# A decay attention and two MLPs on one core: buffers, loads and copies of the attention stage rearranged

## The chip, the cores and the metric

One Trainium2 chip, one of its cores. The metric is the device time of one execution in microseconds, the median of several runs; lower is better. TensorE (PE) multiplies, VectorE (DVE), ScalarE (ACT) and GpSimd (POOL) do the element work, SyncE (SP) issues most transfers. Each engine runs its own instructions in order and waits on semaphores for the others.

## What is computed

Twelve chunks of 64 positions go through a linear attention with decay, for 2 batches and 8 heads; its output is the input of two MLPs of 2048 hidden units. All in float32.

```python
for b in range(nb):                                  # 12 chunks of 64 positions
    intra = (einsum('bhic,bhjc->bhij', qb, kb) * Dmask) @ vb
    inter = einsum('bhid,bhde->bhie', qb * lam_pow, kv_state)
    out[:, :, chunk] = intra + inter
    kv_state = lam_block * kv_state + einsum('bhsd,bhse->bhde', kb * rev_pow, vb)
x = out as (1536 tokens, 512)
h = x @ w_in;  x = (h * clip(h + 3, 0, 6) / 6) @ w_out       # first MLP
h = x @ w_in2; out = maximum(0.01 * h, h) @ w_out2           # second MLP
```

## The kernel before

**Layout.** The two batches lie on the two halves of the partitions: `own[b]` are the 64 partitions of batch b, `other[b]` the rest (lines 155 and 156). The hidden states lie in three groups of 512 tokens, `t` = 0, 1, 2; four chunks of both batches make a group (`SPT` = 4).

**The order.** Nothing is issued as it is written. Each step is added to a list with `add(engine and modelled us, function, due, after, takes, frees)` (line 52). `Order.issue` (line 59) then plays a model of the engines: a step may start when its `after` steps are done in the model, the buffers that it takes are free and its engine is idle; among those that may start, the earliest due goes first, dues being carried back along `after`. The instructions are written in that order, and on the chip each engine keeps it, whatever it waits for. SP's transfers are one such engine ("dma"), so a load that waits for a buffer holds up all loads behind it.

**The attention, chunk by chunk** (lines 242 to 362). `load_qk` brings queries, keys and keys by position, three transfers of 128 partitions, into one of `NQ` = 4 places in the tile `sums`. `load_v` brings the values of two chunks into a tile `vs` (3 buffers) of 128 partitions, two chunks, two slots; both transfers write slot 0 on all 128 partitions. `part_v` then copies the half of batch 1 from slot 0 to slot 1, ScalarE for chunks 0 to 2, VectorE for the others, and `state_copy` puts the running state on the partitions left over, so that one matmul takes values and state at once. `queries` copies queries to PSUM beside the scores (two copies), `scores` is 32 small matmuls, `mask` multiplies by the decay on VectorE, `k_decay` scales keys on GpSimd, `state` and `attn_out` are 32 small matmuls each, and `att_x` splits the output in PSUM into a high part (a cast on ScalarE) and a low part (a difference on VectorE), because the later products take each operand as high and low. A place for queries is free again when scores, query copies and scaled keys of its chunk are done; a value tile when the outputs and states of both of its chunks are done.

**After the attention.** The weights come as raw 64-bit words (`load_w`, 3 buffers) and are turned into high and low parts by ScalarE and VectorE (`low_bits` to `w_low`). The first blocks of the first MLP are done tile by tile. From the third block on, groups 0 and 1 are multiplied by a scheme with seven products instead of eight, which needs differences of the inputs, T1 to T4. `sums_1` (line 877) makes them: `x_whole` (line 620) adds high and low parts back to the whole, four times on VectorE, `x_diff` subtracts, and `x_split` splits again. They lie in a tile of the pool `s`, which opens when the attention's pools close (`open_late`, line 584); the products' sums of weights use the same pool.

Of the kernel before, what the change touches and what calls it, by code (L numbers as in the profile page):

```python
# [40 lines left out]
NQ = 4  # L41
# [75 lines left out]
def decay_attention_two_mlps(ctx: ExitStack, tc: tile.TileContext, qkk, vv, lam, w1, w2, out):  # L117
# [3 lines left out]
    sizes = {"raw": 3, "cv": 3, "cl": 2, "w0": 4, "w1": 5, "st": 2, "G": 3, "u": 3, "h": 2, "a": 2, "r": 3, "vs": 3}  # L121
    late = {"s": 2, "Gx": 3, "ux": 3}
# [125 lines left out]
    def load_v(c):  # L248

        def fn(_):  # L250
            vp = new("vs", [P, 2, 2, H, D], F32)
            VS[c], VS[c + 1] = vp[:, 0], vp[:, 1]
            for i in range(2):
                nc.sync.dma_start(out=vp[:, i, 0], in_=vv[c + i])
            if c == 0:
                nc.gpsimd.memset(vp[other[1], 0, 1], 0.0)
        return fn

    def part_v(c):

        def fn(e):
            (nc.scalar.copy if e == "act" else nc.vector.tensor_copy)(out=VS[c][own[1], 1], in_=VS[c][own[1], 0])  # L262
            if c == 0:
                nc.gpsimd.memset(VS[0][other[0], 0], 0.0)
        return fn
# [62 lines left out]
    x_ready = {}  # L328
    ld = {}
    for c in range(NSC):  # L330
# [3 lines left out]
        ld["v", c] = add(("act", 0.6) if c < 3 else ("dve", 0.5), part_v(c), d - 1.0, after=[ld["vp", c]])  # L334
    st, copies, masks, dense_ops, att_ops = {}, {-1: []}, [], [op_warm], []
    for c in range(NSC):
# [11 lines left out]
        if not last:  # L348
            st[c] = add(pe, state(c), d + 1.3, after=ks + [ld["v", c]] + copies[c - 1] + ([op_rows[c % 2]] if c else []),
                        takes=["a"])  # L350
            copies[c] = [add(("act", 0.58), state_copy(c, b), after=[st[c], ld["v", c + 1]]) for b in range(2)]
            add(("none", 0.0), nothing, after=copies[c], frees=["a"])
        o = add(pe, attn_out(c), d + 2.6, after=[m, ld["v", c]] + copies[c - 1], takes=["h"])
# [5 lines left out]
        x_ready[c] = add(("dve", 0.69), att_x(c, True), d + 5.0, after=[hi], frees=["h"])  # L359
# [86 lines left out]
    composed, low, s_at = {}, {}, {}  # L446
    for l in range(2):
        for f in range(NF):
            for j in range(2):
                h = (l, f, j)  # L450
                held = paired(l, f) and j == 0
                ld_w = add(("dma", 1.45), load_w(h), takes=["raw"])
# [7 lines left out]
            if paired(l, f) and f % 2:  # L460
# [3 lines left out]
                hi = s_at[l, p] = add(("act", 1.05), s_high(l, p), after=[i], takes=["s"])  # L464
# [115 lines left out]
    XT, CS, SPARE = {}, {}, {}  # L580
# [23 lines left out]
    def spare(k, n):  # L604
        i = {"B11": 0, "T1": 0, "B12": 1, "T3": 1, "B22": 2, "T2": 2, "B21": 3, "T4": 3}[n]
        return SPARE[k, 0][:, i] if k else SPARE[k, i // 2][:, i % 2]
# [4 lines left out]
    def x_split(k, n, lo, src):  # L611
# [6 lines left out]
        return fn  # L618

    def x_whole(k, n):  # L620
        def fn(_):
            if n == "B11" or n == "B22" and not k:
                SPARE[k, int(n == "B22")] = pool["s"].tile([P, 2 << k, 2, TT >> k], F32, tag="s", name=f"x_spare{k}")
            x = [part([x[i].bitcast(F32) for x in X], k, n) for i in range(2)]
            nc.vector.tensor_tensor(out=spare(k, n), in0=x[0], in1=x[1], op=ALU.add)
# [249 lines left out]
    last_whole = {}  # L875

    def sums_1(k):
        u, ts = ("dve", 0.61 * (2 - k)), (2, 2) if k else PAIR
        for n, t in (("B11", 0), ("B21", 0), ("B22", 1)):
            x_op[0, k, n] = x_of(ts[t])  # L880
        w = {}
        for n, t in (("B11", 0), ("B12", 1), ("B22", 1), ("B21", 0)):
            w[n] = last_whole[0] = add(u, x_whole(k, n), after=[op_late, last_whole.get(0), *x_of(ts[t])],
                                       takes=["s"] * (n == "B11" or n == "B22" and not k))
        t1 = add(u, x_diff(k, "T1", "B12", "B11", spare), after=[w["B11"], w["B12"]])
        t3 = add(u, x_diff(k, "T3", "B22", "B12", spare), after=[t1, w["B22"]])
# [128 lines left out]
```

## Time and profile before

| | |
|---|---|
| median of 3 runs | 565.16 us (564.86 to 566.2) |
| the profiled execution | 564.53 us |
| its span, first to last instruction | 562.4 us |
| TensorE busy | 548.1 us, 97% |
| VectorE busy | 415.8 us, 74% |
| ScalarE busy | 356.7 us, 63% |
| transfers | 61.66 MB, mean 110 GB/s |
| granted TensorE clock | 0.999 of full speed |

The span is what the trace shows; some 2 us of the execution lie around it. A busy share is a mean over stages with different limits, so the views by stage are read beside it. A timeline row in brackets tells how long the engine sat idle before the instruction and what ended that; "issue" there, and in the chain, is time in which the engine waited for nothing that the profile shows. The DMA share is the mean busy share of the 16 transfer engines; packets that overlap can put it above 1.

### The profile page before, as it was taken

The numbers are of one execution on the slowest core, as the hardware profiler recorded it, in microseconds if no ns is written. First come the engines' busy times: TensorE is split into PE (matmuls) and PEld (weight loads), VectorE is DVE, ScalarE is ACT, GpSimd is POOL, SyncE is SP. The second block draws the span as 40 slices with busy tenths as digits, with TensorE's granted clock in tenths as the row PEclk, the third lists the DMA queues.
The fourth block names the chain that finished last, engine by engine and source line by source line (L and its number), as shares of the span: only waits on it lengthen the run. The fifth ranks groups of instructions, "written<-read, shape, count | busy, mean of one in ns | idle before, by whom it ended". The sixth has DMA issues, their size and how long they took to land.

```text
span 562.4 us, 9066 instructions
## 1 busy us (share of the span) xinstructions
PE 548.1 (97%) x3504; PEld 457.6 (81%) x3504; DVE 415.8 (74%) x693; ACT 356.7 (63%) x625; POOL 68.2 (12%) x78
## 2 busy tenths in 40 slices
PE   8889999999999999999999999999999999999996
PEld 5778888888888888888888888888888888888885
DVE  7868999989888985787689897686368943782332
ACT  5688885658656845578675886686268825683111
POOL 6561001101011101101000000000110110110000
PEclk9999999999999999999999999999999999999999
DMA  8992334247066434534200402141443622512332
GB/s 310 350 334 100 113 112 94 41 133 201 9 160 153 129 81 107 131 113 93 76 1 1 161 27 85 66 150 38 94 87 119 168 59 45 128 46 43 75 76 75
DMA packets 25436, 61.66 MB, mean 110 GB/s; under 512 B 2994, under 2 KB 2994, under 8 KB 25394
## 3 DMA queue, kind: packets, MB, share of 16 engines
q1 hardware_dynamic: 18592, 48.77, 26.2%
q0 software_dynamic: 6480, 11.80, 12.4%
q8 instruction: 27, 0.44, 0.3%
q10 hardware_dynamic: 322, 0.52, 0.3%
q14 instruction: 15, 0.12, 0.1%
HBM read 46.14 MB, written 3.15 MB: 88 GB/s over the span
## 4 chain that ended last, share of the span: by engine, by line
PE 95%; DMA 2%; issue 1%; DVE 1%; SPq 0%; DVEq 0%
PE acc L552 46%; PE h L639 20%; PE a L639 11%; PE h L482 6%; PE a L482 6%; PE h L315 2%; PE a L303 2%; PE pair L278 2%; DMA vs<-vv 2%; PE a L552 1%; DVE sums L565 0%; SPq L245 0%; DVE r L294 0%; DVE vs L262 0%; DVE a L671 0%
## 5 line engine op out<-in xcount | busy, mean ns | idle before, releaser
L525 POOL DMA_DIRECT2D sums<-st x45 | 39.4, 908 | 423.7 <-ACT st L563 408.4
L552 PE MATMUL acc<-Gh,wh 128*128 128x512 f32 x136 | 53.0, 390 | 0.0
L552 PE MATMUL acc<-Gl,wh 128*128 128x512 f32 x136 | 52.9, 389 | 0.0
L552 PE MATMUL acc<-Gh,wl 128*128 128x512 f32 x136 | 52.9, 389 | 0.0
L552 PE MATMUL acc<-wl,Gh 128*128 128x512 f32 x128 | 50.0, 391 | 0.0
L552 PE MATMUL acc<-wh,Gh 128*128 128x512 f32 x128 | 50.0, 391 | 0.0
L552 PE MATMUL acc<-wh,Gl 128*128 128x512 f32 x128 | 49.8, 389 | 0.0
L387 ACT ACTIVATE c<-raw 128x512 uint32<-128x512 uint32 x64 | 42.8, 670 | 6.4 <-DVE t L410 4.6
L410 DVE CUSTOM_DVE_ANT_0 t<-t,c 128x1024 uint16<-128x1024 uint16 x64 | 45.0, 704 | 2.2
L408 DVE SCALAR_TENSOR_TENSOR t<-raw,t 128x512 uint32<-128x512 uint32 x64 | 44.1, 689 | 1.1
L420 DVE TENSOR_TENSOR wl<-t,wh 128x512 fp32r<-128x512 f32 (+1 forms) x64 | 41.4, 652 | 2.2 <-ACT wh L416 2.0
L391 ACT ACTIVATE t<-raw 128x512 f32<-128x512 f32 x64 | 42.8, 669 | 0.0
L511 DVE TENSOR_TENSOR Gl<-u,Gh 128x512 fp32r<-128x512 f32 x32 | 22.1, 689 | 25.7 <-ACT Gh L689 25.5
L416 ACT CAST wh<-t 128x512 fp32r<-128x512 f32 (+1 forms) x64 | 37.7, 594 | 3.6 <-DVE t L410 2.8
L563 ACT COPY st<-acc 128x512 f32<-128x512 f32 x43 | 25.2, 588 | 22.9 <-PE acc L552 16.3
L639 PE MATMUL h<-xh,s 128*128 128x512 f32 x112 | 38.4, 389 | 0.0
L397 DVE TENSOR_SCALAR t<-t 128x512 f32<-128x512 f32 x64 | 27.0, 421 | 14.6 <-ACT t L391 14.6
L695 ACT ACTIVATE u<-a 128x512 f32<-128x512 f32 x24 | 14.3, 597 | 30.9 <-PE a L639 30.9
L565 DVE TENSOR_TENSOR sums<-acc,sums 128x512 f32<-128x512 f32 x27 | 18.5, 690 | 20.3 <-PE acc L552 20.2
L508 DVE SCALAR_TENSOR_TENSOR Gl<-u,Gh 128x512 fp32r<-128x512 f32 x36 | 24.6, 686 | 8.7 <-ACT Gh L501 8.6
L552 PEld LDWEIGHTS acc<-Gh,wh 128*128 128x128 f32 x136 | 25.5, 188 | 5.4
L552 PEld LDWEIGHTS acc<-Gh,wl 128*128 128x128 f32 x136 | 25.5, 188 | 5.4
(181 smaller groups left out, 1482.2 us busy)
## 6 DMA issues: line engine op xcount, KB each, us to landing
raw<-w SPq DMA_DIRECT2D x58, 512.0 KB, 3.3
sums<-st POOLq DMA_DIRECT2D x45, 256.0 KB, 3.9
sums<-qkk SPq DMA_DIRECT2D x36, 256.0 KB, 5.5
vs<-vv SPq DMA_DIRECT2D x12, 256.0 KB, 5.0
raw<-w SPq DMA_DIRECT2D x12, 256.0 KB, 3.7
out<-sums SPq DMA_DIRECT2D x20, 128.0 KB, 2.4
out<-sums ACTq DMA_DIRECT2D x4, 128.0 KB, 3.2
lam_sb<-lam ACTq DMA_DIRECT2D x1, 0.0 KB
```

What stands on the lines that cost most here:

```text
L387: nc.scalar.activation(out=CV[h][1], in_=RAW[h][:, :, 0], func=AF.Copy, scale=2.0 ** -29)
L391: return lambda _: nc.scalar.activation(out=CV[h][0].bitcast(F32), in_=RAW[h][:, :, 1].bitcast(F32), func=AF.Abs)
L397: nc.vector.tensor_scalar(out=t.bitcast(F32), in0=t.bitcast(F32), scalar1=MAG_MIN, scalar2=MAG_MAX, op0=ALU.max, op1=ALU.min)
L408: nc.vector.scalar_tensor_tensor(out=t, in0=RAW[h][:, :, 1], scalar=0xC0000000, in1=t, op0=ALU.bitwise_and, op1=ALU.bitwise_or)
L410: nc.vector.tensor_tensor(out=t, in0=t, in1=c, op=ALU.add)
L416: nc.scalar.copy(out=W[h][0][:, cols(*h)], in_=CV[h][0].bitcast(F32)[:, cols(*h)])
L420: return lambda e: eng[e].tensor_tensor(out=W[h][1][:, cols(*h)], in0=CV[h][0].bitcast(F32)[:, cols(*h)], in1=W[h][0].bitcast(F32)[:, cols ...
L482: nc.tensor.matmul(ps, a[:, ws], x[:, k, :], start=(n == 0), stop=(n == 3 * KC - 1))
L525: return lambda _: nc.gpsimd.dma_start(out=SUM[t][:, e, :], in_=STAGE[t, e], accum_op=ALU.add)
L552: nc.tensor.matmul(ACC[e], a, x, start=(first and n == 0 and not seeded(s, e)), stop=(last and n == 2), skip_group_check=seeded(s, e))
L563: nc.scalar.copy(out=STAGE[t, e], in_=ps)
L639: nc.tensor.matmul(ps, ws[a][:, c * P:(c + 1) * P], xs[b][:, c], start=(first and n == 0), stop=(n == 5), skip_group_check=True)
```

## The change

- `NQ` goes from 4 to 3, the value tiles `vs` from 3 to 2.
- The pool `s` opens at the start instead of after the attention.
- `load_v` writes the half of batch b of both chunks straight into slot b: two transfers of 64 partitions by two chunks, instead of two of 128 partitions. `part_v` goes; what waited for it waits for the load.
- `att_spare` is new: for the chunks of groups 0 and 1 ScalarE copies the attention output in PSUM a second time, whole, into a tile of `s`. The PSUM buffer is free when low part and whole copy are done. `x_whole` goes, and `sums_1` starts from these copies.
- Loads of raw weights are bound behind loads of queries: the first behind chunk 8, the second behind chunk 10, all others behind chunk 11.

The core of the diff:

```diff
@@ -38,7 +38,7 @@
 N_DENSE = {("s", 0): 5, ("t", 0): 2, ("o", 0): 2}
-NQ = 4
+NQ = 3
 
@@ -118,8 +118,8 @@
 
-    sizes = {"raw": 3, "cv": 3, "cl": 2, "w0": 4, "w1": 5, "st": 2, "G": 3, "u": 3, "h": 2, "a": 2, "r": 3, "vs": 3}
-    late = {"s": 2, "Gx": 3, "ux": 3}
+    sizes = {"raw": 3, "cv": 3, "cl": 2, "w0": 4, "w1": 5, "st": 2, "s": 2, "G": 3, "u": 3, "h": 2, "a": 2, "r": 3, "vs": 2}
+    late = {"Gx": 3, "ux": 3}
     const = ctx.enter_context(tc.tile_pool(name="const", bufs=1))
@@ -250,18 +250,10 @@
             VS[c], VS[c + 1] = vp[:, 0], vp[:, 1]
-            for i in range(2):
-                nc.sync.dma_start(out=vp[:, i, 0], in_=vv[c + i])
-            if c == 0:
-                nc.gpsimd.memset(vp[other[1], 0, 1], 0.0)
-        return fn
-
-    def part_v(c):
-
-        def fn(e):
-            (nc.scalar.copy if e == "act" else nc.vector.tensor_copy)(out=VS[c][own[1], 1], in_=VS[c][own[1], 0])
-            if c == 0:
-                nc.gpsimd.memset(VS[0][other[0], 0], 0.0)
+            for b in range(2):
+                nc.sync.dma_start(out=vp[own[b], :, b], in_=vv[c:c + 2, own[b]].rearrange("c p h d -> p c h d"))
+                if c == 0:
+                    nc.gpsimd.memset(vp[other[b], 0, b], 0.0)
         return fn
@@ -325,13 +317,23 @@
 
-    x_ready = {}
+    SPARE = {}
+
+    def att_spare(c):
+        def fn(_):
+            j, i = divmod(c, SPT)
+            if not i:
+                SPARE[j] = pool["s"].tile([P, 2, 2, TT], F32, tag="s", name="x_spare")
+            x = SPARE[j].rearrange("p j k (c b i) -> p (j k) c b i", c=SPT, b=2)[:, :, i]
+            nc.scalar.copy(out=x, in_=PA["o", c])
+        return fn
+
+    x_ready, spared = {}, {}
     ld = {}
...
         ld["vp", c] = ld["vp", c - 1] if c % 2 else add(("dma", 1.4), load_v(c), d if c else 0.0, after=[ld["qk", c]], takes=["vs"])
-        ld["v", c] = add(("act", 0.6) if c < 3 else ("dve", 0.5), part_v(c), d - 1.0, after=[ld["vp", c]])
     st, copies, masks, dense_ops, att_ops = {}, {-1: []}, [], [op_warm], []
@@ -346,17 +348,20 @@
         if not last:
-            st[c] = add(pe, state(c), d + 1.3, after=ks + [ld["v", c]] + copies[c - 1] + ([op_rows[c % 2]] if c else []),
+            st[c] = add(pe, state(c), d + 1.3, after=ks + [ld["vp", c]] + copies[c - 1] + ([op_rows[c % 2]] if c else []),
                         takes=["a"])
-            copies[c] = [add(("act", 0.58), state_copy(c, b), after=[st[c], ld["v", c + 1]]) for b in range(2)]
+            copies[c] = [add(("act", 0.58), state_copy(c, b), after=[st[c], ld["vp", c + 1]]) for b in range(2)]
             add(("none", 0.0), nothing, after=copies[c], frees=["a"])
-        o = add(pe, attn_out(c), d + 2.6, after=[m, ld["v", c]] + copies[c - 1], takes=["h"])
+        o = add(pe, attn_out(c), d + 2.6, after=[m, ld["vp", c]] + copies[c - 1], takes=["h"])
         add(("none", 0.0), nothing, after=[o, st.get(c)], frees=["vs"] * (c % 2) + ["r"])
...
         hi = add(("act", 0.58), att_x(c, False), d + 4.0, after=[o])
-        x_ready[c] = add(("dve", 0.69), att_x(c, True), d + 5.0, after=[hi], frees=["h"])
+        x_ready[c] = add(("dve", 0.69), att_x(c, True), d + 5.0, after=[hi])
+        if c < 2 * SPT:
+            spared[c] = add(("act", 0.58), att_spare(c), d + 5.0, after=[hi], takes=["s"] * (not c % SPT))
+        add(("none", 0.0), nothing, after=[x_ready[c], spared.get(c)], frees=["h"])
         att_ops += [x_ready[c], m, o, *ks, *copies.get(c, []), *([st[c]] if c in st else [])]
@@ -443,13 +448,14 @@
 
-    composed, low, s_at = {}, {}, {}
+    AFTER_QK = {(0, 0, 0): NSC - 4, (0, 0, 1): NSC - 2}
+    composed, low = {}, {}
     for l in range(2):
...
                 held = paired(l, f) and j == 0
-                ld_w = add(("dma", 1.45), load_w(h), takes=["raw"])
+                ld_w = add(("dma", 1.45), load_w(h), after=[ld["qk", AFTER_QK.get(h, NSC - 1)]], takes=["raw"])
                 a = add(("act", 0.67), low_bits(h), after=[ld_w], takes=["cv", "cl"])
@@ -461,7 +467,7 @@
                     i = add(("dve", 0.43), w_sum(l, p, n), after=[composed[l, f - 1, 0], composed[l, f, 0], i])
-                hi = s_at[l, p] = add(("act", 1.05), s_high(l, p), after=[i], takes=["s"])
+                hi = add(("act", 1.05), s_high(l, p), after=[i], takes=["s"])
                 s_ready[l, p] = add(("dve", 1.22), s_low(l, p), after=[hi], frees=["raw"])
@@ -577,7 +583,7 @@
 
-    XT, CS, SPARE = {}, {}, {}
+    XT, CS = {}, {}
     A_B = (("A11", "B11"), ("S1", "T1"), ("S2", "T2"), ("A12", "B21"), ("S3", "T3"), ("S4", "B22"), ("A22", "T4"))
@@ -602,8 +608,8 @@
     def spare(k, n):
-        i = {"B11": 0, "T1": 0, "B12": 1, "T3": 1, "B22": 2, "T2": 2, "B21": 3, "T4": 3}[n]
-        return SPARE[k, 0][:, i] if k else SPARE[k, i // 2][:, i % 2]
+        i = {"B11": 0, "T1": 0, "B21": 1, "T4": 1, "B12": 2, "T3": 2, "B22": 3, "T2": 3}[n]
+        return SPARE[i // 2][:, i % 2]
 
@@ -615,14 +621,6 @@
                 nc.scalar.copy(out=xh, in_=src(k, n))
-        return fn
-
-    def x_whole(k, n):
-        def fn(_):
-            if n == "B11" or n == "B22" and not k:
-                SPARE[k, int(n == "B22")] = pool["s"].tile([P, 2 << k, 2, TT >> k], F32, tag="s", name=f"x_spare{k}")
-            x = [part([x[i].bitcast(F32) for x in X], k, n) for i in range(2)]
-            nc.vector.tensor_tensor(out=spare(k, n), in0=x[0], in1=x[1], op=ALU.add)
         return fn
@@ -872,24 +870,18 @@
 
-    last_whole = {}
-
-    def sums_1(k):
-        u, ts = ("dve", 0.61 * (2 - k)), (2, 2) if k else PAIR
+    def sums_1():
+        u = ("dve", 1.22)
         for n, t in (("B11", 0), ("B21", 0), ("B22", 1)):
-            x_op[0, k, n] = x_of(ts[t])
-        w = {}
-        for n, t in (("B11", 0), ("B12", 1), ("B22", 1), ("B21", 0)):
-            w[n] = last_whole[0] = add(u, x_whole(k, n), after=[op_late, last_whole.get(0), *x_of(ts[t])],
-                                       takes=["s"] * (n == "B11" or n == "B22" and not k))
-        t1 = add(u, x_diff(k, "T1", "B12", "B11", spare), after=[w["B11"], w["B12"]])
-        t3 = add(u, x_diff(k, "T3", "B22", "B12", spare), after=[t1, w["B22"]])
-        t2 = add(u, x_diff(k, "T2", "B22", "T1", spare), after=[t3])
-        t4 = add(u, x_diff(k, "T4", "B21", "T2", spare), after=[t2, w["B21"]])
-        for n, after in (("T1", [t2]), ("T2", [t4]), ("T4", [t4]), ("T3", [t3, last1[0, ts[1]]])):
-            splits(0, k, n, after, spare)
-        done = [x_op[0, k, n][0] for n in ("T1", "T3", "T2", "T4")]
-        for d in (done,) if k else (done[:2], done[2:]):
+            x_op[0, 0, n] = x_of(PAIR[t])
+        t1 = add(u, x_diff(0, "T1", "B12", "B11", spare), after=list(spared.values()))
+        t3 = add(u, x_diff(0, "T3", "B22", "B12", spare), after=[t1])
+        t2 = add(u, x_diff(0, "T2", "B22", "T1", spare), after=[t3])
+        t4 = add(u, x_diff(0, "T4", "B21", "T2", spare), after=[t2])
+        for n, after in (("T1", [t2]), ("T2", [t4]), ("T4", [t4]), ("T3", [t3, last1[0, PAIR[1]]])):
+            splits(0, 0, n, [op_late, *after], spare)
+        done = [x_op[0, 0, n][0] for n in ("T1", "T4", "T3", "T2")]
+        for d in (done[:2], done[2:]):
             add(("none", 0.0), nothing, after=d, frees=["s"])
@@ -964,8 +956,7 @@
 
-    sums_1(0)
-    od.ops[s_at[0, starts[0][SINGLE] // 2]][3].append(last_whole[0])
+    sums_1()
     for b in range(SINGLE, len(BLOCKS[0])):
```

## Rows read from the trace of the kernel before

**Rows 1.** Busy time by stage: stretch, length, each engine, clock, DMA share, GB/s.
```profile
0.00:50.00 50.00, 42.07 (x989) 34.70 (x990) 40.35 (x55) 34.94 (x61) 28.86 (x33) 1.00 0.84 297
50.00:400.00 350.00, 350.00 (x1720) 291.07 (x1719) 289.35 (x489) 243.72 (x421) 25.35 (x29) 1.00 0.34 95
```

**Rows 2.** Chain of waits, 0 to 62 us: start, length in us, what.
```profile
15.69 0.88 issue
...
18.62 1.08 PE a L303 x32
...
20.89 1.66 issue
...
31.18 1.22 issue
...
41.30 0.96 issue
...
42.59 1.08 PE a L303 x32
...
46.59 0.97 issue
...
48.01 2.98 PE h L482 x12
```

**Rows 3.** Timeline of TensorE, one block: start, us, what, idle time before it.
```profile
36.92 0.33 PE L315 MATMUL h<-r,vs 128*64 128x64 f32 x2 [0.28 <-issue]
37.18 1.15 PE L278 MATMUL pair<-sums 64*64 64x64 f32 x32
38.26 1.15 PE L303 MATMUL a<-vs,kd 128*64 128x64 f32 x32
39.24 1.10 PE L315 MATMUL h<-r,vs 128*64 128x64 f32 x32
40.27 1.02 PE L278 MATMUL pair<-sums 64*64 64x64 f32 x27
```

**Rows 4.** The page: busy time, a transfer queue, one line of the DMA issues.
```profile
PE 548.1 (97%) x3504; PEld 457.6 (81%) x3504; DVE 415.8 (74%) x693; ACT 356.7 (63%) x625; POOL 68.2 (12%) x78
...
q8 instruction: 27, 0.44, 0.3%
...
vs<-vv SPq DMA_DIRECT2D x12, 256.0 KB, 5.0
```

**Rows 5.** Busy time by stage again: first loads, stores on one queue, on two.
```profile
2.00:24.00 22.00, 18.59 (x385) 13.64 (x385) 18.10 (x26) 13.71 (x24) 14.04 (x13) 1.00 1.03 371
544.10:545.90 1.80, 1.80 (x12) 1.38 (x11) 0.38 (x1) 0.00 (x0) 0.00 (x0) 1.00 0.95 205
557.80:558.30 0.50, 0.00 (x0) 0.00 (x0) 0.18 (x1) 0.00 (x0) 0.00 (x0) 1.00 1.04 389
```

**Rows 6.** Timeline of SP's transfer queue: start, us to issue, what, how many.
```profile
33.64 0.80 SPq L254 DMA_DIRECT2D vs<-vv  x2
34.48 2.01 SPq L380 DMA_DIRECT2D raw<-w  x2
```

**Rows 7.** Timeline of ScalarE, one chunk in the attention.
```profile
28.12 1.19 ACT L308 COPY vs<-a 64x512 f32<-64x512 f32 x2 [0.48 <-PE a L303]
29.21 0.58 ACT L325 CAST xh<-h 128x512 fp32r<-128x512 f32 x1
29.82 1.20 ACT L286 COPY pair<-sums 64x512 f32<-64x512 f32 x2
```

**Rows 8.** Lines 262 and 625 (ns min/median/max), and a timeline row of TensorE.
```profile
L262 DVE COPY vs<-vs x9: 419/425/1281, 12.7 to 45.6; 64x512 f32<-64x512 f32 x9
L262 ACT COPY vs<-vs x3: 614/616/616, 6.2 to 12.5; 64x512 f32<-64x512 f32 x3
...
L625 DVE TENSOR_TENSOR x_spare<-xh,xl x4: 1217/1220/1220, 63.3 to 97.4; 128x1024 f32<-128x1024 f32 x4
...
9.98 1.15 PE L303 MATMUL a<-vs,kd 64*64 64x64 f32 x32 [0.74 <-POOL kd L268]
```


## What the change is expected to do

> **What bounds the kernel now.** I read the table by stage first. From 50 to 400 us TensorE is busy in all 350.00 of 350.00 us, in 0 to 50 us only 42.07 of 50 [rows 1]. What the change does to VectorE, ScalarE and the loads can therefore move the end only through the first 50 us, where 7.9 us lie open. Everything after is a fixed train of matmuls, which starts earlier or later.
>
> Next I read the chain of waits of that stretch. It shows where the open time lies: the chain runs over TensorE alone, and the holes are called "issue", 0.88, 1.66, 1.22, 0.96 and 0.97 us [rows 2], with one of 0.28 more [rows 3], together 5.97 us. No semaphore explains them, and they fall inside groups of 32 equal matmuls whose operands are all there. So I counted matmuls between two holes: 2 + 32 + 32 + 32 + 27 = 125 [rows 3], with a weight load each 250 instructions. TensorE runs 2 x 3504 instructions, and the queue called instruction carries 27 packets with 0.44 MB [rows 4], 16 KB and 260 instructions a packet. The match says that each hole is a wait for the next block of TensorE's own code, which comes over the same transfer engines as the data. This is inferred from the count; no row names it. The Trainium skill, "Runtime: NRT & Kernel Launch", section on instruction fetch mechanics, describes such refills in blocks of 16 KiB or 256 instructions and calls the crossing mostly hidden; the 0.28 to 1.66 us here speak against the second half.
>
> Why the code is late: from 2 to 24 us the transfer engines move 371 GB/s at a share of 1.03, so a 16 KB packet stands behind data [rows 5]. TensorE's own step (scores, state, outputs of one chunk) is 40.27 - 37.18 = 3.09 us [rows 3]; from the state products at 18.62 to those at 42.59 six steps pass, 4.00 us each [rows 2]. The attention runs at the pace of its code.
>
> **The change, part by part.** The sum is made against the profiled execution, 564.53 us with a span of 562.4; it is 0.63 us under the median of 565.16, and I add the difference to the median.
>
> *Sums of tokens.* Four adds of 1.22 us leave VectorE, 4.9 us, between 63 and 99 us [rows 8]. TensorE has no open time there, so they are worth 0; the cover is the 350 us without a hole. If it were gone, they would be worth at most 4.9 us. In their place ScalarE gets eight copies of 128x512 from PSUM during the attention; the nearest row is the cast of the same tile, 0.58 us [rows 7], together 4.6 us. Three copies of 0.62 us leave ScalarE, 1.8 us [rows 8].
>
> *ScalarE's step.* Now it has 1.19 (state copies) + 0.58 (cast) + 1.20 (queries) = 2.97 us a chunk [rows 7]; with the new copy 3.55. That is more than TensorE's 3.09 and less than the 4.00 that a step takes. Where a code wait lengthens a step, the copy hides in it; where none does, ScalarE sets the step and 0.46 us are lost. With a block of 125 matmuls for each 96 of a step, about two of seven steps have no long wait: 2 x 0.46 = 0.9, of which I take half, 0.5, since a neighbouring wait takes up some. The ends are 0 and 7 x 0.46 = 3.2. The copy also holds a PSUM buffer of the outputs longer; the next output but one needs it, a step later, so that costs 0.
>
> *Values.* Nine copies leave VectorE (median 0.425, longest 1.281 us) and three leave ScalarE [rows 8]. No hole of the chain ends at one, so they are worth 0 in the steady steps. At the start GpSimd no longer waits for such a copy before it clears a half and scales keys, and the state products waited 0.74 us for those keys [rows 8]. That bounds the gain by 0 and 0.74; I take 0.2, because the keys need the decay table too, which VectorE finishes at about the same time.
>
> *Half-partition loads.* The values now come as 64 partitions by two chunks. No load of that shape is in the trace; the nearest rows are the output stores from 64 partitions. Halves issued in turn on one queue moved 205 GB/s at a share of 0.95, both halves from two queues 389 at 1.04 [rows 5]. Taken over to the loads, 12 x 256 KB = 3.15 MB need 15.3 us instead of 3.15 / 371 = 8.5, 6.8 us more of transfer time; the other end is 0 more. I take the first. It is hidden: 9.44 MB of queries and keys (25.4 us at 371), the values (15.3) and two slices of weights (1.05 MB, 2.8) end at 2 + 43.5 = 45.5 us, and TensorE needs the last of them only at the train that starts at 48.01 [rows 2]. The Trainium skill, "SBUF — State Buffer", section on the DMA port swizzle, says the same against this change: 64 partitions reach half of the ports, 196 GB/s instead of 328; the stores agree, no load here shows it. Its next section has two halves in flight at once gain 6% only; here they gain 90%, and the measurement stands.
>
> *Fewer buffers.* Three instead of four for queries and keys, two pairs instead of three for values. A value load waited for the outputs two pairs of chunks before; now it waits for one pair later. The load of chunks 8 and 9 would go when that of 10 and 11 went, 33.64 [rows 6], and its first reader, the state product at 42.59 [rows 2], comes 8.95 us after. Landing takes 5.0 us at the median [rows 4], 1.1 more at half rate: 2.8 us to spare. Behind that load on SP's queue stand the queries of 9 and 10 and a weight slice; scores of 10 come after 42.59 too. So 0, and up to 2 us if SP's order is worse.
>
> *Raw weights behind.* A slice already goes at 34.48, directly behind the values of 10 and 11, whose queries went before them [rows 6]; the slice ahead of it is bound to the queries of 8, which are due far earlier than any weight. The constraint repeats that order: 0.
>
> *Code waits.* What matters most has no row of its own. Before, 13.6 MB kept the engines at 1.03 until 24 us; after, fewer loads are queued at a time, but each pair of values holds the engines 1.1 us longer, and they stay busy until 45. The first shortens the waits, the second lengthens them. The ends are -4.5 and +3.2 (rivals below); I take 0.
>
> Sum: 0.5 - 0.2 = +0.3 us; 564.53 becomes 564.8, and the median 565.16 becomes **565.5**.
>
> **The rivals.** *Slower: code waits under half-rate values.* Place: the four holes from 31 us on, where engines that had pauses are now busy. Price: 1.22, 0.28, 0.96 and 0.97 (3.43) grow to the longest seen, 1.66 each (6.64): +3.2, 568.4 us. It decides as soon as the values' packets hold the engines at half rate while queries queue behind them. For it: 205 against 389 GB/s. Against it: a slower pace gives the engines gaps again. The page on SBUF named above would make this the outcome if its rate holds for loads.
>
> *Faster: the shorter queue lets the code through.* With a buffer less of each kind less data is queued ahead of a code packet. If the waits vanish, ScalarE's 3.55 us set the step: 6 x (4.00 - 3.55) = 2.7, with the first and last hole (0.88 and 0.97 [rows 2]) 4.5. I price it between, -3.4: 561.8 us. For it: the longest hole, 1.66 at 20.89, falls where the share is 1.03. Against it: holes of 0.96 and 0.97 remain at 41 and 46 us, where the big rush is over.
>
> *Nothing moves.* The added copies hide in the code waits wholly, the rest under busy TensorE: 565.2.
>
> **How the numbers follow.** Forecast (564.3 to 567.0) 0.36, nothing 0.08, slower rival (566.9 to 569) 0.26, faster rival (560.5 to 563.4) 0.30. About 0.3%, 1.7 us, is what a measurement here can tell from no change. Faster: 0.30 and a sliver of the forecast, 0.31; slower: 0.26 and some of the forecast above 566.9, 0.29; same 0.40. Signs are mixed, so the likeliest case's own range stands above; the range for 8 in 10 cuts the outer part of both rivals: 561.2 to 568.6.
>
> **What would show it.** In the profile after: value loads at about half the rate, share near 1 until some 45 us; holes "issue" on TensorE every 125 matmuls, of 6 us together (4 or less for the faster rival, 8 or more for the slower); ScalarE's step about 3.55 us where no hole falls; the train starting within 1.5 us of 48.01; 350 us of 350 busy after it. The prediction fails if a load is waited for in the steady steps, if ScalarE's added copies delay the state copies in every step, or if TensorE has holes between 50 and 400 us.

## The result, and the profile after

The changed kernel takes **568.85 us** (median of 5 runs, 567.9 to 569.52) where the kernel before, run beside it, takes 564.97 (5 runs, 564.65 to 566.2): a ratio of 1.0063, 95% interval 1.0047 to 1.0080. It is slower, by 3.88 us. The forecast was 565.5, and the upper end of the range, 568.6, lies 0.25 below. The profiled execution took 569.27 us with a span of 567.5, against 564.53 and 562.4.

The table by stage of the kernel after (stretch, length, busy time and count of TensorE, its weight loads, VectorE, ScalarE and GpSimd, clock, DMA share, GB/s):

```profile
0.00:50.00 50.00, 39.41 (x910) 32.38 (x912) 30.87 (x41) 32.82 (x58) 26.49 (x32) 0.97 0.93 268
2.00:24.00 22.00, 18.99 (x331) 13.70 (x331) 14.67 (x21) 11.06 (x20) 12.74 (x13) 0.92 1.02 283
12.00:14.00 2.00, 1.30 (x33) 0.97 (x32) 1.97 (x3) 1.92 (x4) 0.98 (x1) 1.00 1.09 193
20.00:22.00 2.00, 2.00 (x40) 1.88 (x38) 1.41 (x2) 1.14 (x4) 0.93 (x2) 0.50 1.06 229
50.00:400.00 350.00, 349.46 (x1779) 290.42 (x1775) 286.51 (x486) 247.94 (x427) 25.55 (x29) 1.00 0.35 97
```

Set beside [rows 1, 5]: after 50 us TensorE is still busy, 349.46 of 350.00, so the loss lies in the first 50 us, as the frame of the prediction had it. There two columns have changed. From 2 to 24 us the engines move 283 GB/s where they moved 371, at the same share (1.02, before 1.03): they are as busy and carry less. And the granted clock is 0.92 there, 0.50 from 20 to 22 us, which is the 1.2 GHz level; before it was 1.00.

The page of the profile gives the same for single loads (KB each, median us from issue to landing):

```profile
sums<-qkk SPq DMA_DIRECT2D x36, 256.0 KB, 6.6
vs<-vv SPq DMA_DIRECT2D x12, 256.0 KB, 7.1
```

A value load takes 7.1 us to land, 5.0 before [rows 4]. The loads of queries, whose shape the change leaves alone, land late as well: 6.6 us, where the page of the kernel before has

```profile
sums<-qkk SPq DMA_DIRECT2D x36, 256.0 KB, 5.5
```

The records of single packets, which the trace keeps, say it most plainly: from 12 to 14 us a packet of 2 KB takes 0.172 us at the median, in the same stretch of the kernel before 0.087.

What that does to the engines is read from ScalarE's timeline, and from TensorE's, of the kernel after (start, us, what, idle time before it):

```profile
12.82 1.20 ACT L278 COPY pair<-sums 64x512 f32<-64x512 f32 x2
17.18 1.20 ACT L278 COPY pair<-sums 64x512 f32<-64x512 f32 x2 [3.16 <-DMA sums<-qkk]
18.41 1.18 ACT L300 COPY vs<-a 64x512 f32<-64x512 f32 x2
```

```profile
16.81 0.97 PE L270 MATMUL pair<-sums 64*64 64x64 f32 x25 [0.56 <-issue]
19.09 0.30 PE L295 MATMUL a<-vs,kd 128*64 128x64 f32 x2 [1.31 <-issue]
19.64 1.71 PE L295 MATMUL a<-vs,kd 128*64 128x64 f32 x30 [0.26 <-ACT vs L300]
21.28 1.97 PE L270 MATMUL pair<-sums 64*64 64x64 f32 x32
23.19 1.23 PE L307 MATMUL h<-r,vs 128*64 128x64 f32 x32
...
26.37 0.98 PE L295 MATMUL a<-vs,kd 128*64 128x64 f32 x27 [1.83 <-issue]
...
36.18 2.08 PE L270 MATMUL pair<-sums 64*64 64x64 f32 x64 [1.13 <-ACT pair L278]
...
41.07 0.33 PE L307 MATMUL h<-r,vs 128*64 128x64 f32 x2 [0.79 <-issue]
...
48.00 0.34 PE L295 MATMUL a<-vs,kd 128*64 128x64 f32 x5 [2.09 <-issue]
```

ScalarE waits 3.16 us for the queries of chunk 3. The copies of the state stand behind them in its queue, so they begin at 18.41, and the state products of chunk 2 begin at 19.09, when the first of them has ended (18.41 + 0.58 = 18.99). That hole of 1.31 us bears the name "issue", but the time of the copy tells whose it is; in the trace TensorE's wait for ScalarE's semaphore ends at 19.03. Then the clock is halved: 30 state products take 1.71 us and 32 scores 1.97 us, against 1.15 for 32 of either before [rows 3].

**Where the 5 us of the span went.** All holes of TensorE up to 60 us make 10.0 us. In the kernel before they made 6.7, the 5.97 of "issue" and 0.74 for the keys [rows 2, 3, 8]: +3.3. Which of them are waits for code, the names in the brackets do not tell. The packet records do: in both kernels each hole that the prediction reads as a code wait ends 1.24 to 1.51 us after a 16 KB packet of the queue called instruction has landed. In the kernel after these are the holes of 0.56, 1.83, 0.79 and 2.09 us named "issue" and the one of 1.13 at 36.18, whose packet landed at 34.94 (the copy in its bracket had ended at 35.36). That makes 6.4 us, or 6.8 with a hole of 0.41 at 30.91 where a packet and a copy both fit, against 5.97 before. No such packet landed between 15.49 and 24.88 us, so the hole at 19.09 is not one of them. The other holes, waits for loads and for other engines, grew from 0.7 to between 3.2 and 3.6 us; the 1.31 above is the largest. The slow stretch costs some 1.5 us more: from 19.64 to 24.25 us TensorE does 94 matmuls in 4.61 us, and at the pace of [rows 3] they take 30/32 x 1.08 + 1.08 + 1.03 = 3.1. Together +4.8 of the +5.1 in the span. The train of the first MLP starts at 50.28 instead of 48.01 [rows 2], with more of the attention still to do behind it. Behind the attention nothing more is lost: the 1200th matmul, at 72.40 us, begins 5.34 us later than in the kernel before, the 3500th 5.30.

### The profile page after: what moved, and what is told of

Its sections match the earlier page's. It is cut to its first block, busy times and chain, and to the rows that moved or that the text cites. A ratio compares the mean times of both kernels' runs of the same rounds, so it can differ in the third digit from the quotient of the medians.

```text
span 567.5 us, 9057 instructions
## 1 busy us (share of the span) xinstructions
PE 550.2 (97%) x3504; PEld 459.0 (81%) x3504; DVE 406.0 (72%) x680; ACT 360.2 (63%) x630; POOL 67.8 (12%) x78
## 4 chain that ended last, share of the span: by engine, by line
PE 90%; DMA 6%; SPq 1%; ACT 1%; DVE 1%; issue 1%; DVEq 0%; ACTq 0%
PE acc L558 45%; PE h L637 20%; PE a L637 11%; PE a L488 6%; PE h L488 5%; DMA vs<-vv 2%; DMA raw<-w 2%; DMA sums<-qkk 1%; PE a L558 1%; PE h L307 1%; PE pair L270 1%; SPq L245 0%; ACT pair L278 0%; ACT vs L300 0%; PE a L295 0%
## 5 line engine op out<-in xcount | busy, mean ns | idle before, releaser
L558 PEld LDWEIGHTS acc<-Gl,wh 128*128 128x128 f32 x136 | 25.5, 188 | 5.2
```

The lines of the kernel that those rows point to most:

```text
L558: nc.tensor.matmul(ACC[e], a, x, start=(first and n == 0 and not seeded(s, e)), stop=(last and n == 2), skip_group_check=seeded(s, e))
```

## The experiments

Theory A, formed from the trace above: the loads of values on 64 partitions halve the rate of the transfer engines, the queries behind them come late, TensorE falls idle and then runs at the lower clock. Rivals: the loss comes from fewer buffers or from SP's order; from the whole copies on ScalarE; from code waits that grew. The change has four parts that act in the first 50 us, and the runs put them together in different ways. "Places" are those of queries and of value pairs; the ratio is to the kernel before in the same series (its medians 564.97, 564.82, 564.50 and 564.58). Ratio and interval come from all runs of a series, so they can differ a little from the quotient of the two medians.

| run | values on | places | weights bound | whole copies | us | ratio, 95% interval |
|---|---|---|---|---|---|---|
| after | 64 | 3, 2 | yes | yes | 568.85 | 1.0063, 1.0047 to 1.0080 |
| e1 | 128 | 3, 2 | yes | yes | 565.14 | 1.0005, 0.9990 to 1.0020 |
| e6 | 128 | 4, 3 | yes | yes | 565.24 | 1.0022, 1.0003 to 1.0041 |
| e11 | 128 | 3, 2 | yes | no | 564.09 | 0.9986, 0.9970 to 1.0002 |
| e4 | 128 | 3, 2 | no | no | 567.72 | 1.0048, 1.0032 to 1.0064 |
| e3 | 64 | 4, 3 | no | no | 575.21 | 1.0187, 1.0156 to 1.0218 |
| e5 | 64 | 3, 2 | yes | no | 570.31 | 1.0111, 1.0052 to 1.0171 |
| e7 | 64 | 3, 2 | no | yes | 570.77 | 1.0111, 1.0095 to 1.0128 |

**One: the values as before.** The changed kernel, with the old loads and the copies of a half:

```diff
-            for b in range(2):
-                nc.sync.dma_start(out=vp[own[b], :, b], in_=vv[c:c + 2, own[b]].rearrange("c p h d -> p c h d"))
+            for i in range(2):
+                nc.sync.dma_start(out=vp[:, i, 0], in_=vv[c + i])
...
+        ld["v", c] = add(("act", 0.6) if c < 3 else ("dve", 0.5), part_v(c), d - 1.0, after=[ld["vp", c]])
```

> The changed kernel with the old value loads put back: two transfers of 128 partitions, and the copy of batch 1's half to its slot. All else stays changed (three and two buffers, whole tokens copied by ScalarE, weights behind). Theory H, half-rate value loads are the cost: the DMA rate from 2 to 24 us goes back from 283 to about 370 GB/s, the clock stays full, and the time falls by most of the 3.9 us lost, to 565 to 566. Theory Q, a value load that waits for one of two buffers holds the queries behind it on SP: the time stays within 1 us of 568.9, and the transfer engines still lie idle around 28 us. Theory S, ScalarE's added copies: stays at 568.9 or above, since ScalarE gets three copies more.

565.14 us: the whole loss is gone. By stage:

```profile
2.00:24.00 22.00, 20.27 (x435) 15.25 (x433) 18.87 (x26) 15.39 (x28) 14.01 (x13) 1.00 0.87 293
```

The rate is hardly above the 283 of the kernel after, but at a share of 0.87: here the engines have pauses, because the loads wait for places, and what is asked for comes in time. So GB/s alone prove nothing; it is the rate at a full share that fell. The clock is at 2.4 GHz throughout.

**Two: the halves from two queues.** In the changed kernel the half of batch 1 is issued by ScalarE:

```diff
-                nc.sync.dma_start(out=vp[own[b], :, b], ...
+                (nc.scalar if b else nc.sync).dma_start(out=vp[own[b], :, b], ...
```

> The changed kernel with the values of batch 1 loaded through ScalarE's transfer queue and those of batch 0 through SP's as before, so that both halves of the partitions can be in flight at once, as the two stores at the end of the kernel before were at 389 GB/s. Theory H: the DMA rate from 2 to 24 us rises from 283 to above 330 GB/s and the time falls by 1 to 3 us; ScalarE pays six transfer issues of about 0.5 us and may wait for a value buffer at them, which takes part of it back. Theory Q or S: no gain, 569 or above.

572.78 us, ratio 1.0140 (1.0104 to 1.0175): slower still. ScalarE issues its halves where they stand in its own queue: the first three lie 0.8, 1.2 and 3.5 us away from SP's, so the start of the run is no clean test of halves in flight together. Two pairs are, which both queues issue at one moment, at 28.57 and at 37.30 us. The stretches behind the first are

```profile
30.00:32.00 2.00, 1.08 (x38) 0.94 (x34) 1.66 (x2) 1.92 (x4) 1.57 (x2) 1.00 1.00 252
32.00:34.00 2.00, 2.00 (x72) 1.93 (x69) 1.33 (x2) 1.88 (x4) 0.54 (x1) 1.00 1.11 243
```

About 250 GB/s at a full share; behind the second pair, from 40 to 42 and from 42 to 44 us, it is 206 and 259. The stores' 389 GB/s from two queues [rows 5] are not had for these loads.

**Three: the straight loads alone**, in the kernel before (the edit of one, the other way round):

> The kernel before with the value loads straight to place as its only change (four and three buffers, sums of tokens on VectorE). Theory H: 567 to 569, 2 to 4 us slower than the kernel before, with a DMA rate below 300 GB/s from 2 to 24 us. Theory Q or S: within 1 us of 565, or a little faster for the twelve copies that go.

575.21 us, +10.4 against the kernel before, where Theory H had 2 to 4: the half-partition loads alone cost more than the whole change. Stage and largest holes:

```profile
2.00:24.00 22.00, 18.62 (x332) 13.90 (x332) 14.30 (x21) 9.87 (x18) 10.46 (x12) 0.93 1.04 266
```

```profile
19.82 1.15 PE L270 MATMUL pair<-sums 64*64 64x64 f32 x32 [2.64 <-ACT pair L278]
...
35.68 0.27 PE L295 MATMUL a<-vs,kd 128*64 128x64 f32 x1 [2.06 <-issue]
...
42.43 2.42 PE L295 MATMUL a<-vs,kd 128*64 128x64 f32 x31 [4.47 <-issue]
```

Same picture as after, and larger: 266 GB/s at 1.04, a wait for queries, then holes named "issue". The last matmuls run 31 in 2.42 us, again at the 1.2 GHz level, behind 4.47 us of idleness. That longest hole has a reason of its own, on ScalarE:

```profile
41.07 0.66 ACT L378 ACTIVATE c<-raw 128x512 uint32<-128x512 uint32 x1 [4.73 <-DMA raw<-w]
41.75 1.18 ACT L300 COPY vs<-a 64x512 f32<-64x512 f32 x2
```

ScalarE waits 4.73 us for a weight slice on the slow stream, and the copies of the state stand behind that step. This may be part of why the loads cost 10.4 us alone and less in the changed kernel, where the weights are bound behind the queries; no run parts it off.

**Four: fewer places alone**, in the kernel before:

```diff
-NQ = 4
+NQ = 3
-    ... "r": 3, "vs": 3}
+    ... "r": 3, "vs": 2}
```

> The kernel before with only its buffers changed: three places for queries and keys, two for values. Theory Q: 566.5 to 569, transfer engines idle where SP waits for a value buffer, holes in TensorE that are waits for queries. Theory H or S: within 1 us of 565; shorter queues may even shorten the code waits and give 563 to 565.

567.72 us, +2.9. SP's queue tells why:

```profile
7.79 8.15 SPq L245 DMA_DIRECT2D sums<-qkk  x9
15.99 0.90 SPq L380 DMA_DIRECT2D raw<-w  x2
17.00 0.84 SPq L254 DMA_DIRECT2D vs<-vv  x2
```

In the planner's model no value tile is free at that point, so a weight slice goes ahead of the values, at 15.99 us; in the kernel before the first one goes at 26.76. TensorE then has a hole of 2.48 us that ends at 22.27, and the clock is 0.50 from 22 to 24 us. By the packet records this hole is a wait for code (a 16 KB packet landed 1.53 us before its end). That the time lost goes back to the weights ahead in the queue is shown by run eleven, not by this trace.

**Five: without the whole copies.** The kernel before with straight loads, fewer places and bound weights; the sums of tokens stay on VectorE:

> The changed kernel without the whole-token copies: the four adds on VectorE come back, ScalarE has no second copy of the output; straight loads, three and two buffers and weights behind stay. Theory H (half-rate loads are the cost, the copies are hidden): within 1.5 us of the 568.9 of the changed kernel. Theory S (ScalarE's 3.55 us a chunk cost something): 1 us or more faster, 567.5 or less. The reverse, 570 or more, would say that the copies bring something that I did not count.

570.31 us, four runs between 566.99 and 574.29. That is too wide to say whether the copies bring something, as the expectation has it for 570 or more. It says one thing: even at the lower end of its interval, 1.0052, the kernel without the copies is 2.9 us over the kernel before, so they are not what most of the 3.88 comes from.

**Six: old value loads, and four and three places** in the changed kernel:

> The changed kernel with the old value loads and with four places for queries and three value tiles, so that only the whole-token copies and the weights behind the queries are left of the change. The first run series put the old value loads back with three and two buffers at 565.1. Theory Q (few buffers cost 2.9 us, as they did alone): 562 to 563.5, faster than both kernels. Theory S: 565 to 567, since the copies and three more on ScalarE set the step. If the weights behind already cure what few buffers cost: 564.5 to 565.5.

565.24 us, 1.0022 (1.0003 to 1.0041): no better than e1. More places bring nothing where the weights are bound and the loads use all partitions.

**Seven: the weights free** in the changed kernel:

```diff
-                ld_w = add(("dma", 1.45), load_w(h), after=[ld["qk", AFTER_QK.get(h, NSC - 1)]], takes=["raw"])
+                ld_w = add(("dma", 1.45), load_w(h), takes=["raw"])
```

> The changed kernel with the raw weights not bound behind the queries. The prediction called this constraint worth 0. With only the buffers changed, SP put a weight slice at 15.99 us, before the queries of chunk 5. Theory O (the constraint matters once queries must wait for a place, because weights then slip ahead): 570 to 573, weight slices before 25 us. Theory of the prediction: within 1 us of 568.9.

570.77 us, 6.27 over the kernel before of its series, where the changed kernel was 3.88 over: 2.4 us more. The weight slices go at 14.82 and 24.27 us. The binding, which I had put down at nothing, is worth that much.

**Eight: less data.** The kernel before, with the third transfer of queries and keys (keys by position) left out for chunks 4 to 11, so that part of what is computed uses old keys:

```diff
-            for i in range(3):
+            for i in range(3 if c < NQ else 2):
```

> The kernel before, with one of three transfers (the keys by position) left out for chunks 4 to 11, which use those of the chunk four earlier: 2.1 of 13.6 MB less, all else in place, so its output is not that of the reference. Theory C (the holes called issue are waits for TensorE's code behind data): the holes after 20 us, 5.1 us together, shrink to 3 or less, and the train of matmuls at 48.0 starts 1.5 to 3 us earlier, 562 to 563.5. Rival: the holes have another cause (an operand that the trace does not name): they keep their size, and the time stays at 564.5 to 565.3.

562.12 us, 0.9962 (0.9947 to 0.9977). TensorE's holes from 20 us on:

```profile
21.39 1.08 PE L278 MATMUL pair<-sums 64*64 64x64 f32 x29 [0.56 <-issue]
30.14 0.22 PE L303 MATMUL a<-vs,kd 128*64 128x64 f32 x1 [0.40 <-issue]
35.49 0.33 PE L315 MATMUL h<-r,vs 128*64 128x64 f32 x2 [1.10 <-issue]
41.10 0.34 PE L278 MATMUL pair<-sums 64*64 64x64 f32 x5 [1.23 <-issue]
```

3.29 us where the kernel before has 1.66 + 1.22 + 0.28 + 0.96 + 0.97 = 5.09 [rows 2, 3]. The holes stay at the same kind of place, inside groups of equal matmuls, and shrink when 2.1 MB less are moved. Each of the four ends 1.28 to 1.57 us after a 16 KB packet of the queue called instruction has landed, so they are waits for code; that the packets come late because data is ahead of them rests on the shrinking. The train starts 2.4 us earlier than in the kernel before, as Theory C of this run has it.

**Nine: the queries first.** Is it only the order, or the rate? In the changed kernel each value pair after the first goes behind the queries of the next chunk too, and queries keep the order of the chunks:

```diff
-    ... load_v(c), d if c else 0.0, after=[ld["qk", c]], takes=["vs"])
+    ... load_v(c), d if c else 0.0, after=[ld["qk", min(c + 1, NSC - 1) if c else 0]], takes=["vs"])
```

> The changed kernel with one difference: the loads of queries go in the order of the chunks, and each pair of value loads after the first goes behind the queries of the next chunk too (chunk 3's queries go ahead of the values of 2 and 3, chunk 5's ahead of those of 4 and 5). The value loads keep their half of the partitions and the buffers their number. Theory A (the loss lies in the order: ScalarE waits for the queries of chunk 3 until 17.18 us, the copies of the state stand behind them, TensorE idles 1.31 + 0.26 us and then runs some 4 us at the 1.2 GHz level, about 1.75 us more): the queries of 3 are copied before 16 us, that hole closes, the clock stays at 2.4 GHz there, and the time falls by 2 to 3.3 us, to 565.5 to 567. Theory B (the loss is the transfer time that 64-partition loads take, whoever stands first): the wait moves from the queries to the values, an equal hole stands before state products or outputs, and the time is 568 to 570.

569.63 us, 1.0082 (1.0056 to 1.0107). ScalarE, then TensorE:

```profile
13.33 2.42 ACT L278 COPY pair<-sums 64x512 f32<-64x512 f32 x4
15.78 1.19 ACT L300 COPY vs<-a 64x512 f32<-64x512 f32 x2
```

```profile
18.52 0.30 PE L295 MATMUL a<-vs,kd 128*64 128x64 f32 x2 [1.07 <-POOL kd L260]
19.87 1.94 PE L295 MATMUL a<-vs,kd 128*64 128x64 f32 x30 [1.06 <-DVE r L286]
21.74 1.74 PE L270 MATMUL pair<-sums 64*64 64x64 f32 x32
```

The queries of chunk 3 are there: four copies run without a wait from 13.33, and the state copies end at 16.97. Still the same state products begin only at 18.52 and go on at 19.87. The two halves of their values were issued at 10.57 and 11.24, and by the trace's semaphore records, where TensorE waits for each of them, they landed at 18.38 and 19.74: both starts follow 0.13 to 0.14 us behind. The names in the brackets are of other steps; the keys of that chunk, for one, were done at 16.07. The wait moved from the queries to the values, 1.57 us of hole became 2.13, and the clock fell as before. Theory B of this run holds: the rate, not the order.

**Ten: the hole filled.** Five matmuls of zeros stand ahead of the state products of chunk 2 in the changed kernel:

```diff
             ps = PA["t", c] = new("a", [P, H, D], F32)
+            for _ in range(5 if c == 2 else 0):
+                nc.tensor.matmul(ps.rearrange("p h d -> p (h d)"), zeros[:, :P],
+                                 zeros.unsqueeze(1).to_broadcast([P, 2, TT // 2]), start=True, stop=True)
```

> The changed kernel with five matmuls of zeros, 128x512 each, put ahead of the state products of chunk 2, where TensorE idles from 17.8 to 19.1 us; they need no data that comes late. Output and loads are unchanged. If the slow products between 19.64 and 23.2 us (1.71 and 1.97 us for 30 and 32 matmuls, 1.08 and 1.15 at full clock) are paid for by the idle time before them: the granted clock stays at 2.4 GHz there and the time falls by up to 1.75 us, to 567.1. If the clock falls for another reason (more idle time elsewhere), the products stay slow and the time is that of the changed kernel, 568.9, or up to 1 us above it for the added matmuls.

570.26 us, 1.0096 (1.0068 to 1.0124), eight runs from 567.01 to 574.57; the interval overlaps that of the changed kernel. TensorE:

```profile
17.53 1.25 PE L293 MATMUL a<-zeros 128*128 128x512 bf16 x5
18.82 0.30 PE L298 MATMUL a<-vs,kd 128*64 128x64 f32 x2
19.38 1.15 PE L298 MATMUL a<-vs,kd 128*64 128x64 f32 x30 [0.26 <-ACT vs L303]
20.46 1.15 PE L270 MATMUL pair<-sums 64*64 64x64 f32 x32
22.20 1.15 PE L310 MATMUL h<-r,vs 128*64 128x64 f32 x32 [0.60 <-DVE r L286]
25.66 1.15 PE L298 MATMUL a<-vs,kd 128*64 128x64 f32 x32 [2.30 <-issue]
26.61 1.87 PE L310 MATMUL h<-r,vs 128*64 128x64 f32 x32
28.41 1.92 PE L270 MATMUL pair<-sums 64*64 64x64 f32 x32
```

The local half of the expectation came true: with 0.26 us of idle time ahead of them, not 1.57, the same products take 1.15 and 1.15 us instead of 1.71 and 1.97. The gain is not kept. TensorE arrives earlier at its next wait, which is one for code (its packet landed at 24.24, in the kernel after at 24.88), idles 2.30 us there instead of 1.83, and pays the lower clock behind that hole, 1.87 and 1.92 us. What comes over the transfer engines sets the pace, and a faster stretch of TensorE only moves the wait.

**Eleven: fewer places, and the weights bound**, in the kernel before (e4 with the binding of the change):

> The kernel before with three places for queries, two value tiles, and the loads of raw weights bound behind the queries as in the change; values still come on 128 partitions and are copied, no whole copies of the output. With the buffers alone the time was 567.72, with a weight slice ahead of the values at 15.99 us. Theory A (what the buffers cost is that the weights slip ahead on SP's queue): the binding brings it back to that of the changed kernel with the old value loads, 565.0 to 565.6. Theory B (a load that waits for one of fewer buffers holds the queue up by itself): 567 to 568, binding or not.

564.09 us, 0.9986 (0.9970 to 1.0002), 0.49 under the kernel before where e4 was 2.90 over: 3.4 us back. This is 0.9 us below the range of this run's Theory A and far from that of Theory B: what fewer places cost is the weights that slip ahead.

```profile
2.00:24.00 22.00, 19.39 (x435) 14.88 (x433) 18.79 (x26) 14.40 (x26) 14.05 (x14) 1.00 0.95 329
```

**Twelve: one transfer for three.** The kernel before with queries, keys and keys by position of a chunk in one transfer of 768 KB:

```diff
-            for i in range(3):
-                nc.sync.dma_start(out=QK[c % NQ][:, i], in_=qkk[c, :, i])
+            nc.sync.dma_start(out=QK[c % NQ], in_=qkk[c])
```

> The kernel before with queries, keys and keys by position of a chunk in one transfer of 768 KB instead of three of 256 KB; nothing else differs. SP issues 12 transfers for 36. If the length of what is queued ahead of the blocks of TensorE's code counts, this moves nothing or puts the first queries later, since one transfer is complete only when all three parts are there: 565 to 567. If SP's issuing delays the loads (0.5 to 1 us for each of them between 7.99 and 25.74 us), the later chunks come earlier and the time falls to 562.5 to 564, which would be under both kernels.

565.94 us, 1.0009 (0.9994 to 1.0024): no difference in time, which speaks against a cost of SP's issuing. It does not rule one out. In the profiled run TensorE ends the scores begun at 40.31 at 41.46, 1.1 us ahead of the kernel before (42.59), and then loses it again in a hole and at the 1.2 GHz level:

```profile
43.56 1.15 PE L302 MATMUL a<-vs,kd 128*64 128x64 f32 x32 [2.10 <-ACT wh L415]
44.51 1.71 PE L314 MATMUL h<-r,vs 128*64 128x64 f32 x32
```

By the packet records that hole is a wait for code too (landed at 42.04, 1.52 us before its end). No version that does the whole work beats the kernel before: e11 comes nearest, and its interval holds 1.

## Why the prediction was right or wrong

**The frame held.** The end moved only through the stretch in which the attention runs, some 60 us in the kernel after, and the train behind kept its length. The sums of tokens are worth nothing, as said: VectorE lost their time and TensorE's 349.46 us of 350 do not show it.

**Half-partition loads: the step that failed is "it is hidden".** Size and sign of the slowness were right: 205 GB/s at 0.95, taken from the stores [rows 5], and the loads show 193 at 1.09 from 12 to 14 us. That it costs nothing was wrong: it costs 3.6 us in the changed kernel (3.88 less the 0.32 of e1). The Trainium skill, "SBUF — State Buffer", section on the DMA port swizzle, gives 196 GB/s for 64 partitions; the trace now agrees for loads as well. The 90% by which two halves in flight gain, which the prediction set against that page, are the stores' alone: the loads of e2 moved 206 to 259 GB/s where the stores moved 389. The ledger was wrong in kind. It added up all bytes, let them end at 45.5 us and compared that with the train at 48.01. But the queries of every chunk have a time of their own by which they are needed, from the first 10 us on, and they stand on one queue behind the value pairs. Six of the twelve value loads are issued by 17.2 us. A total that ends in time says nothing on chunk 3. Nor did it end in time: the loads also wait for places, and SP issues the last value pair only at 47.05. Undoing this part alone takes back the whole loss (e1), and doing it alone loses 10.4 us (e3). That the loss is that of the rate, not of the order of two loads, is shown by e9.

**The clock was not in the sum at all.** A hole was priced at its own length. Here a hole brought 1.5 us of matmuls at the 1.2 GHz level, and in the trace of e10 the two belong together: no hole there, no slow matmuls. It also shows that this is no separate loss of 1.5 us to be won back, since the next wait took it.

**Fewer buffers: 0 was right by luck of another part.** Alone they cost 2.9 us (e4), above the "up to 2 us if SP's order is worse" that I kept as an end. The order did get worse, by a weight slice at 15.99, which I had not looked for: I checked when a value load may go, not what the planner puts in its place while it may not.

**Raw weights behind: "repeats that order" was wrong.** It repeats the order of the kernel before, but fewer places would have changed that order. The binding is what makes the fewer places free: 3.4 us between e4 and e11, 2.4 us between e7 and the changed kernel. Two parts that I priced one by one at nothing are +2.9 and -3.4, and only together come near 0.

**ScalarE's step and the copies** were sized well. Cast, whole copy, state and query copies take 0.58 + 0.58 + 1.18 + 1.20 = 3.54 us by the trace, forecast 3.55. With whole loads and bound weights the kernel with the copies stands at 1.0005 (e1), without them at 0.9986 (e11): 0.8 us apart against the kernel before of their series, with intervals that overlap, and the forecast was +0.5. Whether it is 0 or 1 us stays open. The gain of 0.2 us at the start is not seen: the first state products no longer wait for keys, but the outputs ahead of them wait 0.17 us for values, and the next state products 0.70 for keys.

**Code waits: taken as unchanged, 5.97 us, and they are 6.4 to 6.8.** That they are waits for code, which the prediction inferred from a count, the packet records show; that less data shortens them, e8. The **slower rival** gave 568.4 us against 568.85. Its condition came true word for word, "the values' packets hold the engines at half rate while queries queue behind them", but its place was wrong, and that its price comes so near is luck. It let the four code waits from 31 us on grow from 3.43 to 6.64; the ones from there on are 4.0, or 4.4 with the 0.41. What grew more was waiting for data and for what stands behind it, from 9 us on, and with it came the lower clock. I gave it 0.26 because the ledger seemed to cover the data. The **faster rival** is dead: with the shorter queue and full-rate loads (e11) the time does not fall by 3.4 us.

**The signs that I had named**: half rate of the value loads, yes; the share near 1 until some 45 us, yes but for a pause (0.48 from 26 to 30 us); 350 us busy, yes; code holes of about 6 us, yes; the train within 1.5 us of 48.01, no, 50.28. And the first of the failures I listed, a load that is waited for in the steady steps, is what happened.

## What to carry to other kernels

A transfer that covers half of the partitions saves a copy on an engine and here moved at about half the rate, and everything queued behind it paid as well: before such a swap, look whether the DMA share is at 1 in the stretch where the load is issued. Check a load ledger against the time of each consumer in queue order, never against the end of the stage. And when buffers become fewer, ask which transfer the planner puts into the gap: bind the ones that are not urgent behind the ones that are.

## What the runs showed of the hardware that was not expected

- Loads on 64 partitions slow the whole stream, not themselves alone. From 12 to 14 us of the kernel after the engines move 193 GB/s at a share of 1.09. The same stretch of the kernel before, with both kinds of loads on 128 partitions, reads as below. No run parts the 64 partitions from the pattern of two chunks that these loads also have; the packets are 2 KB in both kernels.

```profile
12.00:14.00 2.00, 2.00 (x39) 1.31 (x36) 1.26 (x2) 1.08 (x2) 1.85 (x3) 1.00 1.06 389
```

- Two halves on two queues, issued at one moment, reach 206 to 259 GB/s as loads (e2) where stores reached 389 [rows 5]. Why loads differ from stores was not settled.
- TensorE's code comes in 16 KB packets over the same transfer engines. In the kernels before and after TensorE goes on 1.24 to 1.51 us after the one that it waits for has landed, whatever name the hole bears.
- A hole in TensorE's work may be followed by matmuls at the 1.2 GHz level, and its length alone does not tell. Behind the 1.83 us at 26.37 and the 2.09 us at 48.00 of the kernel after the matmuls run at full pace, behind 2.30 us in e10 and the holes between 16 and 19.6 us in the kernel after they do not.
